# The first batch's chunk pairs interleaved in one pipeline, with idle products at the start and casts spread over engines

## The chip, the cores and the metric

The kernel runs on one core of one Trainium2 chip. The metric is device time in microseconds (us) of one execution; the figure given is the median of several runs. The core's engines work side by side, each through its own instructions in order: PE (TensorE, matrix products; PEld are its weight loads), DVE (VectorE), ACT (ScalarE), POOL (GpSimd) and SP, which here issues nearly all transfers (DMA).

## The reference

Four batches, 8 heads, 768 time steps, heads of 64. The first half is a retention layer (a linear attention with decay), the second a mixer with phases:

```python
gamma = 1.0 - 2.0 ** (-5.0 - np.arange(H))
for t in range(S):
    state = gamma * state + einsum('bhd,bhe->bhde', k[:, :, t], v[:, :, t])
    y[:, :, t] = scale * einsum('bhd,bhde->bhe', q[:, :, t], state)
x = y.transpose(0, 2, 1, 3).reshape(B, S, H * D)          # 4 x 768 x 512
theta = x @ w_theta
zr, zi = x * cos(theta), x * sin(theta)
u = x + einsum('ts,bsd->btd', w_tok_r, zr) + einsum('ts,bsd->btd', w_tok_i, zi)
out = u + maximum(u @ w_ch, 0)
```

## The kernel before

Time is cut into chunks of 128 steps: 6 a batch, 24 in all. Within a chunk the retention is a masked product; across chunks it is a running state. Chunk n's work has these stages, named as in the code:

- `prep`: k is cast to bf16, q and v are scaled by the decay (tiles kqb, vb), on POOL.
- `T`: PE transposes k and q (kq_ps), DVE copies them to kqT.
- `A`: PE forms the scores at_ps, DVE multiplies them with the mask into at. There is one at_ps buffer, so the next A waits for this mask.
- `Y`: PE multiplies at with v into yT_ps, and adds the product of the state (stbd) with q; the state's own product goes to st_ps, which ACT copies to stbd. ACT copies yT_ps to xT.
- `X`: PE transposes xT back (x_ps; DVE copies it to x_sb) and forms theta (th_ps); ACT takes cosine and sine (cs).
- `Z`: DVE forms z = x * (cos, sin).

When z of all six chunks of a batch is there, `moe_M` forms u for each of six output tiles (y_ps), `moe_U` transposes u, and `moe_O` multiplies with w_ch and stores. `w_cast` (POOL) casts a strip of both token weights to bf16 (wrow, three buffers), `w_tok` transposes it on PE (w_ps) and DVE and ACT copy it to wtr and wti.

The first batch is handled in three pairs of chunks: `load_pair` fetches 256 steps at once, two neighbouring steps to a row, and `pair_prep`, `pair_T`, `pair_A` and `pair_Y` take the place of the stages above; `two` counts the even and odd steps of a pair, `a` its two chunks. In `pair_Y` the two chunks' state products and readings are done one after the other. The other batches run one chunk to a slot, in the loop over `s_` at the end, with parts of `moe_M`, `moe_U` and `moe_O` between.

The order of the work on each engine is the order in which the code is written, since no scheduler moves anything (`manual_schedule`). Loads are queued in the order of one string, `loads("p0 th p1 w0 p2 w1 w2 c6 ...")` (p a pair, c a chunk, w a strip of the token weights, th and ch the two other weights); a load whose buffer is still in use holds up all behind it. PSUM has eight banks: two for at_ps, two with the tag "tr" (all transposes), two "acc" (yT_ps, th_ps, o_ps), one "y" (y_ps), one "st" (the state).

Of the kernel before, what the change touches and what calls it, by code (L numbers as in the profile page):

```python
# [14 lines left out]
FT = mybir.dt.float32  # L15
BF = mybir.dt.bfloat16
AF = mybir.ActivationFunctionType
# [4 lines left out]
def _bcast_last(ap: bass.AP, n: int) -> bass.AP:  # L22
    return bass.AP(tensor=ap.tensor, offset=ap.offset, ap=list(ap.ap) + [[0, n]])
# [9 lines left out]
def kernel(  # L33
# [17 lines left out]
    nc = tc.nc  # L51
    B, H, S, D = q.shape
    dm = H * D
    P = 128
    HP = P // 2
    nT = S // P
# [36 lines left out]
    wdma = {}  # L93
# [26 lines left out]
    loads("p0 th p1 w0 p2 w1 w2 c6 w3 c7 ch c8 w4 c9 c10 w5 c11 c12")  # L120


    posn = const.tile([P, nT], FT)
    nc.gpsimd.iota(posn, pattern=[[P, nT]], base=1, channel_multiplier=1,
                   allow_small_or_imprecise_dtypes=True)
# [22 lines left out]
    nc.scalar.activation(vscp, argp, AF.Exp, bias=zerob, scale=-1.0)  # L148
    qscp = const.tile([P, nT, H], FT)
    nc.scalar.activation(qscp, argp, AF.Exp, bias=lscale, scale=1.0)  # L150
    ident = const.tile([P, P], BF)
    make_identity(nc, ident)
    mask = const.tile([P, P], BF)
# [58 lines left out]
    def pair_prep(g, name):  # L212
        t = work.tile([P, 2, dm], BF, name="kqb", bufs=5)
        src = raw[g, name].rearrange("p h (two d) -> p two h d", two=2)
        dst = t.rearrange("p two (h d) -> p two h d", h=H)
        if name == "k":
            nc.gpsimd.tensor_copy(dst, src)
        else:
            for two in range(2):
                sc = (qscp if name == "q" else vscp)[:, 2 * g + two]  # L220
                nc.gpsimd.tensor_mul(dst[:, two], src[:, two], _bcast_last(sc, D))
        st[g, name] = t

    def pair_T(g, name):
        ps = psum.tile([P, NP, 2, P], BF, name="kq_ps", tag="tr", bufs=2)
        for two in range(2):
            for j in range(NP):
                nc.tensor.transpose(ps[:, j, two, :],
                                    st[g, name][:, two, j * P:(j + 1) * P], ident)
        t = work.tile([P, NP, 2, P], BF, name="kqT", bufs=4)  # L230
        nc.vector.tensor_copy(t, ps)
        st[g, name + "T"] = t
# [16 lines left out]
                             _bcast_mid(maskp[:, two].rearrange("p w i -> p (w i)"), H))  # L249
        st[g, two] = at  # L250

    def pair_Y(g):
        yT = [psum.tile([P, NP, P], FT, name="yT_ps", tag="acc", bufs=2)
              for _ in range(2)]
        for two in range(2):
            at, vp = st[g, two], st[g, "v"]
            for j in range(NP):
                for a in range(2):
                    half = slice(a * HP, (a + 1) * HP)
                    for par in range(2):  # L260
                        h = 2 * j + par
                        nc.tensor.matmul(yT[a][par * D:(par + 1) * D, j, :],
                                         vp[half, two, h * D:(h + 1) * D],
                                         at[half, par, j, :],
                                         start=(two == 0 and j == 0),
                                         stop=(g == 0 and a == 0 and two == 1
                                               and j == NP - 1),
                                         skip_group_check=True)
        for a in range(2):
            c = 2 * g + a  # L270
            half = slice(a * HP, (a + 1) * HP)
            if c > 0:
                for j in range(NP):
                    nc.tensor.matmul(yT[a][:, j, :], stbd[c % 2][:, j, :],
                                     st[g, "qT"][:, j, :, half], start=False,
                                     stop=(j == NP - 1), skip_group_check=True)
            if c < nT - 1:
                if c == 0:
                    st_ps[0] = psum.tile([P, NP, P], FT, name="st_ps", tag="st", bufs=1)
                for two in range(2):  # L280
                    for j in range(NP):
                        nc.tensor.matmul(st_ps[0][:, j, :],  # L282
                                         st[g, "k"][half, two, j * P:(j + 1) * P],
                                         st[g, "v"][half, two, j * P:(j + 1) * P],
                                         start=(c == 0 and two == 0 and j == 0),
                                         stop=(c == nT - 2 and two == 1 and j == NP - 1),
                                         skip_group_check=True)
                state_out(0, c)
            if c == 0:
                x_tiles(0)  # L290
            xT = work.tile([P, NP, P], BF, name="xT", bufs=3)
            nc.scalar.copy(xT.rearrange("e j (i w) -> e j w i", w=2),
                           yT[a].rearrange("e j (w i) -> e j w i", w=2))
            st[c] = dict(xT=xT)

    def state_out(b, c):
        for par in range(2):
            sl = slice(par * D, (par + 1) * D)
            nc.scalar.copy(stbd[(c + 1) % 2][sl, :, sl], st_ps[b][sl, :, sl])  # L299

    def x_tiles(b):
        xs[b] = big.tile([P, nT, dm], BF, name="x_sb")
        zs[b] = big.tile([P, nT, 2, dm], BF, name="z")
# [81 lines left out]
    def att_Z(n):  # L385
        b, c = divmod(n, nT)
        nc.vector.tensor_mul(zs[b][:, c], st[n]["cs"], _bcast_mid(xs[b][:, c, :], 2))  # L387
# [57 lines left out]
    def w_cast(t0):  # L445
        for r in range(2):
            row = work.tile([P, S], BF, name="wrow", bufs=3)
            nc.gpsimd.tensor_copy(row, wdma[r, t0])  # L448
            wrow[r, t0] = row

    def w_tok(t0):
        for r in range(2):
            w_ps = psum.tile([P, nT, P], BF, name="w_ps", tag="tr", bufs=2)
            for s0 in range(nT):
                nc.tensor.transpose(w_ps[:, s0, :],
                                    wrow[r, t0][:, s0 * P:(s0 + 1) * P], ident)
            dst = wT[r][:, :, t0 * P:(t0 + 1) * P]
            if r:
                nc.scalar.copy(dst, w_ps)
            else:  # L460
                nc.vector.tensor_copy(dst, w_ps)
# [47 lines left out]
                out=out[b, t0 * P:(t0 + 1) * P, e * hw:(e + 1) * hw], in_=ot)  # L509


    def pair_in(g):
        pair_prep(g, "k")
        pair_T(g, "k")
        pair_prep(g, "q")
        if g > 0:
            att_Z(2 * g - 1)
        pair_T(g, "q")
        pair_prep(g, "v")
        pair_A(g, 0)  # L520
        pair_A(g, 1)
        pair_Y(g)

    pair_in(0)
    nc.vector.tensor_copy(wth, wdma["th"])
    att_X(0)
    att_X(1)
    att_Z(0)
    pair_in(1)
    w_cast(0)  # L530
    att_X(2)
    w_tok(0)
    att_X(3)
    moe_M(0, 0, 2)
    att_Z(2)
    pair_in(2)
    moe_M(0, 2, 4)
    w_cast(1)
    att_X(4)
    w_tok(1)  # L540
    att_X(5)
    w_cast(2)
    att_prep(nT)
    moe_M(1, 0, 4)
    att_Z(4)
    moe_M(0, nT - 2, nT - 1)
    moe_M(1, nT - 2, nT - 1)
# [25 lines left out]
    for s_ in range(last_slot):  # L573
        n = n_of.get(s_)
        if n is not None and n + 5 < NCH and n >= nT + 2:
            load_chunk(n + 5)
        if U_at.get(s_, 0) >= M_DMA:
            moe_U_dma(U_at[s_])
        if n is not None and nT < n < N_DMA:
            att_T(n)  # L580
        if s_ - 3 in n_of:
            att_Z(n_of[s_ - 3])
        hs = halves.get(s_, [])
        if hs:
            moe_M(*hs[0])
        if s_ == 0:
            w_cast(3)
        if s_ in (2, 4):
            w_cast(3 + s_ // 2)
        if s_ + 1 in n_of and n_of[s_ + 1] < N_DMA:  # L590
            att_prep(n_of[s_ + 1])
        if s_ + 2 in n_of and n_of[s_ + 2] >= N_DMA:
            att_prep(n_of[s_ + 2])
            att_T_dma(n_of[s_ + 2])
        if U_at.get(s_, M_DMA) < M_DMA:
            moe_U(U_at[s_])
        if U_at.get(s_ - 1, 0) >= M_DMA:
            moe_O(U_at[s_ - 1])
        if s_ - 1 in n_of:
            att_Yinter(n_of[s_ - 1])  # L600
        if n is not None:
            att_A(n)
        if s_ - 1 in n_of:
            att_Y(n_of[s_ - 1])
            if n_of[s_ - 1] >= N_DMA:
                att_X_dma(n_of[s_ - 1])
        if s_ == 2:
            wch_cast(0, nD)
        if len(hs) > 1:
            moe_M(*hs[1])  # L610
        if s_ in O_at:
            moe_O(O_at[s_])
        if 1 < U_at.get(s_, M_DMA) < M_DMA:
            moe_O(U_at[s_])
        if s_ in (1, 3, 5):
            w_tok(3 + s_ // 2)
        if s_ - 2 in n_of:
            att_X(n_of[s_ - 2])
    moe_last(last_m)
# [28 lines left out]
```

## Time and profile before

| | us |
|---|---|
| median of 3 runs | 200.23 (200.01 to 200.25) |
| the profiled execution's own time | 199.73 |
| its span, first to last instruction | 197.9 |
| PE busy | 166.2 (84%) |
| DVE busy | 105.5 (53%) |
| ACT busy | 76.2 (39%) |
| POOL busy | 77.0 (39%) |

The span is what the profile shows instruction by instruction; the execution's own time is 1.83 us longer. Busy shares are means over the whole span. The page also cuts the span into 40 slices of 4.95 us and gives for each the busy share of every engine and the clock that PE was granted, in tenths of full speed.

### The profile page before, as it was taken

Reading aid. Unit: us, or ns where it says so; the run is one execution under the profiler, and the core shown is the slowest. Engines: PE = TensorE matmul, PEld = TensorE weight load, DVE = VectorE, ACT = ScalarE, POOL = GpSimd, SP = SyncE. Lnnn points to the kernel's source line nnn. Section 1 sums busy time; section 2 is a strip of 40 time slices with the busy share of each in tenths; the row PEclk is TensorE's granted clock in tenths of the full one; section 3 lists DMA queues with packets and bytes.
Section 4 is the critical chain, followed back from the end, with each engine's and each line's share of the span. In section 5 each row is a group of like instructions: output and inputs, shape, how many; then the busy total and the mean of one; then the engine's idle time right before and its main releaser. Section 6 shows DMA issues by size and latency. Waiting matters only on the chain.

```text
span 197.9 us, 3797 instructions
## 1 busy us (share of the span) xinstructions
PE 166.2 (84%) x1508; PEld 96.4 (49%) x1508; DVE 105.5 (53%) x147; ACT 76.2 (39%) x142; POOL 77.0 (39%) x107
## 2 busy tenths in 40 slices
PE   0448628945998997997999999999999999999990
PEld 0335416534554564654565566555555444444460
DVE  1162570462136747776787668666565554543451
ACT  4005703621531577536464464425643353200010
POOL 6849680300189882999255526525000000000000
PEclk9999985596799999999999999999999999999997
DMA  5999995199589999999496886994457445233343
GB/s 152 325 308 336 319 308 140 16 255 283 139 192 226 286 190 227 251 255 229 96 227 129 176 197 151 191 209 106 113 134 74 106 106 108 81 119 107 96 133 108
DMA packets 85906, 35.64 MB, mean 180 GB/s; under 512 B 70912, under 2 KB 80384, under 8 KB 85888
## 3 DMA queue, kind: packets, MB, share of 16 engines
q1 hardware_dynamic: 85744, 35.27, 76.5%
q8 instruction: 12, 0.20, 0.4%
q10 hardware_dynamic: 144, 0.13, 0.2%
q14 instruction: 6, 0.05, 0.1%
HBM read 25.69 MB, written 6.29 MB: 162 GB/s over the span
## 4 chain that ended last, share of the span: by engine, by line
PE 73%; DVE 11%; ACT 6%; DMA 3%; issue 2%; POOL 1%; DVEq 0%; SPq 0%; ACTq 0%; POOLq 0%
PE y_ps L405 29%; PE o_ps L433 10%; PE th_ps L376 10%; DVE at L247 4%; DMA pair<-in_q_dram 3%; PE yT_ps L340 3%; PE at_ps L311 3%; PE x_ps L373 2%; PE st_ps L282 2%; DVE z L387 2%; PE kq_ps L198 2%; PE st_ps L348 2%; DVE at L315 2%; ACT stbd L299 2%; PE at_ps L243 2%
## 5 line engine op out<-in xcount | busy, mean ns | idle before, releaser
L405 PE MATMUL y_ps<-z,wtr 128*128 128x512 bf16 x138 | 52.8, 383 | 1.0 <-DVE z L387 0.6
L405 PE MATMUL y_ps<-z,wti 128*128 128x512 bf16 x138 | 52.8, 383 | 0.0
L381 ACT ACTIVATE cs<-th_ps,halfpi 128x512 bf16<-128x512 f32 x24 | 16.5, 687 | 36.0 <-PE th_ps L376 36.0
L387 DVE TENSOR_TENSOR z<-cs,x_sb 128x1024 bf16<-128x1024 bf16 x24 | 19.7, 822 | 16.1 <-ACT cs L382 16.1
L376 PE MATMUL th_ps<-wth,xT 128*128 128x512 bf16 x96 | 27.3, 411 | 0.0
L299 ACT CAST stbd<-st_ps 64x256 bf16<-64x256 f32 x40 | 14.6, 366 | 30.3 <-PE st_ps L282 29.9
L315 DVE TENSOR_TENSOR at<-at_ps,mask 128x1024 bf16<-128x1024 f32 x18 | 21.9, 1219 | 5.7 <-PE at_ps L311 5.6
L433 PE MATMUL o_ps<-wch,uT 128*128 128x512 bf16 x92 | 23.4, 379 | 0.3 <-ACT cs L382 0.3
L410 DVE TENSOR_TENSOR u<-y_ps,x_sb 128x512 bf16<-128x512 f32 x23 | 15.8, 690 | 12.1 <-PE y_ps L405 12.0
L189 POOL TENSOR_TENSOR vb<-vf,vsc 128x512 bf16<-128x512 f32 x18 | 19.2, 1065 | 6.1 <-PE yT_ps L340 5.0
L436 DVE SCALAR_TENSOR_TENSOR ot<-o_ps,u 128x512 f32<-128x512 f32 x23 | 15.8, 690 | 9.8 <-PE o_ps L433 9.7
L405 PEld LDWEIGHTS <-wti 128*128 128x128 bf16 x138 | 13.6, 98 | 15.2 <-issue 2.4
L448 POOL CAST wrow<-wtok 128x768 bf16<-128x768 f32 x12 | 9.8, 823 | 28.7 <-issue 27.2
L405 PEld LDWEIGHTS <-wtr 128*128 128x128 bf16 x138 | 13.6, 98 | 13.6 <-issue 0.3
L187 POOL TENSOR_TENSOR kqb<-qf,qsc 128x512 bf16<-128x512 f32 x18 | 19.6, 1092 | 0.0
L186 POOL CAST kqb<-kf 128x512 bf16<-128x512 f32 x18 | 11.4, 634 | 19.0 <-issue 14.1
L379 DVE COPY x_sb<-x_ps 128x512 bf16<-128x512 bf16 x19 | 7.9, 418 | 18.0 <-PE x_ps L373 18.0
L382 ACT ACTIVATE cs<-th_ps,zerob 128x512 bf16<-128x512 f32 x24 | 16.3, 680 | 0.0
L356 ACT CAST xT<-yT_ps 128x512 bf16<-128x512 f32 x18 | 10.6, 586 | 11.9 <-PE yT_ps L340 11.7
L201 DVE COPY kqT<-kq_ps 128x1024 bf16<-128x1024 bf16 x13 | 9.0, 691 | 9.3 <-PE kq_ps L198 9.3
L433 PEld LDWEIGHTS <-uT 128*128 128x128 bf16 x92 | 8.8, 98 | 10.3 <-issue 0.6
L376 PEld LDWEIGHTS <-xT 128*128 128x128 bf16 x96 | 9.5, 107 | 8.0 <-issue 2.1
(73 smaller groups left out, 196.0 us busy)
## 6 DMA issues: line engine op xcount, KB each, us to landing
out_dram<-ot SPq DMA_DIRECT2D x23, 256.0 KB, 2.2
kf<-in_k_dram SPq DMA_DIRECT2D x18, 256.0 KB, 4.6
qf<-in_q_dram SPq DMA_DIRECT2D x18, 256.0 KB, 5.1
vf<-in_v_dram SPq DMA_DIRECT2D x18, 256.0 KB, 4.9
wtok<-in_moe_w_tok_r_dram SPq DMA_DIRECT2D x6, 384.0 KB, 5.4
wtok<-in_moe_w_tok_i_dram SPq DMA_DIRECT2D x6, 384.0 KB, 5.2
pair<-in_k_dram SPq DMA_DIRECT2D x3, 512.0 KB, 8.2
pair<-in_q_dram SPq DMA_DIRECT2D x3, 512.0 KB, 9.1
```

Of the source, the lines that this page charges most:

```text
L187: nc.gpsimd.tensor_mul(qb.rearrange(r3, h=H), raw[n, "qf"], _bcast_last(qsc[:, c], D))
L189: nc.gpsimd.tensor_mul(vb.rearrange(r3, h=H), raw[n, "vf"], _bcast_last(vsc[:, c], D))
L299: nc.scalar.copy(stbd[(c + 1) % 2][sl, :, sl], st_ps[b][sl, :, sl])
L315: nc.vector.tensor_mul(at.rearrange("p a j t -> p (a j) t"), at_ps.rearrange("p a j t -> p (a j) t"), _bcast_mid(mask, H))
L376: nc.tensor.matmul(th_ps, s["xT"][:, j, :], wth[:, j, :], start=(j == 0), stop=(j == NP - 1))
L381: nc.scalar.activation(cs[:, 0, :], th_ps, AF.Sin, bias=halfpi, scale=1.0)
L382: nc.scalar.activation(cs[:, 1, :], th_ps, AF.Sin, bias=zerob, scale=1.0)
L387: nc.vector.tensor_mul(zs[b][:, c], st[n]["cs"], _bcast_mid(xs[b][:, c, :], 2))
L405: nc.tensor.matmul(y_ps, wT[r][:, s0, t0 * P:(t0 + 1) * P], zs[b][:, s0, r, :], start=(s0 == 0 and r == 0), stop=(s0 == nT - 1 and r == 1))
L410: nc.vector.tensor_add(u, y_ps, xs[b][:, t0, :])
L433: nc.tensor.matmul(o_ps, mo[m]["uT"][:, j, :], wch[:, j, :], start=(j == 0), stop=(j == nD - 1))
L436: nc.vector.scalar_tensor_tensor(ot, o_ps, 0.0, mo[m]["u"], ALU.max, ALU.add)
```

## The change

1. Fourteen products of a zero tile (`warm`, 128x512) are put at PE's start; their result is not used. DVE clears the tile with its first instruction.
2. A single sine on one column (`sin0`) is put behind the exponentials, so that ACT loads its sine table there.
3. k of a pair is cast on ACT instead of POOL; q's first half is scaled on DVE, its second still on POOL; w_theta is cast on POOL instead of DVE.
4. `pair_Y` is split: `pair_Y(g, two)` has the products with v of one half, `pair_I` the state's reading, `pair_S` the state's product, `pair_out` the copy to xT. They are written in another order, S and Y of a pair between its two masks, and `att_X`, `att_Z` and `moe_M` of earlier chunks stand between the stages of the next pair.
5. In the slots `w_tok` stands ahead of `att_Yinter`, `att_A` and `att_Y` instead of behind them, and `moe_U` behind `att_Yinter`.

```diff
-    pair_in(0)
-    nc.vector.tensor_copy(wth, wdma["th"])
+    warm_ps = psum.tile([P, dm], FT, name="y_ps", tag="y", bufs=1)
+    for _ in range(14):
+        nc.tensor.matmul(warm_ps, warm[:, 0:P], warm, start=True, stop=True)
+    pair_k(0)
+    pair_q(0)
+    pair_prep(0, "v")
+    pair_A(0, 0)
+    nc.gpsimd.tensor_copy(wth, wdma["th"])
+    pair_A(0, 1)
+    pair_S(0, 0)
+    pair_Y(0, 0)
+    pair_S(0, 1)
+    pair_I(0, 1)
+    pair_Y(0, 1)
+    pair_out(0, 0)
+    pair_out(0, 1)
+    pair_k(1)
     att_X(0)
+    pair_q(1)
     att_X(1)
     att_Z(0)
-    pair_in(1)
+    pair_prep(1, "v")
+    pair_A(1, 0)
+    att_Z(1)
     w_cast(0)
+    pair_A(1, 1)
+    pair_S(1, 0)
+    pair_Y(1, 0)
+    pair_I(1, 0)
+    pair_I(1, 1)
+    pair_S(1, 1)
+    pair_Y(1, 1)
+    pair_out(1, 0)
+    pair_out(1, 1)
+    pair_prep(2, "k")
     att_X(2)
+    att_X(3)
     w_tok(0)
-    att_X(3)
+    pair_T(2, "k")
     moe_M(0, 0, 2)
+    pair_q(2)
     att_Z(2)
-    pair_in(2)
-    moe_M(0, 2, 4)
+    pair_prep(2, "v")
+    pair_A(2, 0)
+    moe_M(0, 2, 3)
+    att_Z(3)
     w_cast(1)
+    pair_A(2, 1)
+    pair_S(2, 0)
+    pair_Y(2, 0)
+    pair_I(2, 0)
+    pair_I(2, 1)
+    moe_M(0, 3, 4)
+    pair_Y(2, 1)
+    pair_out(2, 0)
+    pair_out(2, 1)
+    w_tok(1)
     att_X(4)
-    w_tok(1)
-    att_X(5)
     w_cast(2)
     att_prep(nT)
     moe_M(1, 0, 4)
+    att_X(5)
     att_Z(4)
...
+        if s_ in (1, 3, 5):
+            w_tok(3 + s_ // 2)
...
         if s_ - 1 in n_of:
             att_Yinter(n_of[s_ - 1])
+        if U_at.get(s_, M_DMA) < M_DMA:
+            moe_U(U_at[s_])
```

`pair_k(g)` is `pair_prep(g, "k")` and `pair_T(g, "k")`, and `pair_q(g)` the same for q. The new casts:

```diff
         if name == "k":
-            nc.gpsimd.tensor_copy(dst, src)
...
+            nc.scalar.copy(dst, src)
+        for two in range(2):
+            if name == "q":
+                eng = (nc.vector, nc.gpsimd)[two]
...
```

ACT from its last exponential to the sines of the first two chunks, before. The buffer's number stands behind each name; xT_328 and xT_344 are chunks 0 and 1.

```order
L150 ACTIVATE qscp_189<-argp_185,lscale_171 128x48
L299 CAST stbd1_207<-st_ps_315 64x4x64 x2
L292 CAST xT_328<-yT_ps_281 128x4x2x64
L299 CAST stbd0_205<-st_ps_315 64x4x64 x2
L292 CAST xT_344<-yT_ps_282 128x4x2x64
L381 ACT_TABLE_LOAD
L381 ACTIVATE cs_358<-th_ps_352,halfpi_173 128x512
```

The same place after the change; kqb_232 and kqb_366 are k of the first and the second pair.

```order
L152 ACTIVATE qscp_191<-argp_187,lscale_173 128x48
L154 ACT_TABLE_LOAD
L154 ACTIVATE sin0_193<-zerob_177 128x1
L221 CAST kqb_232<-pair_72 128x1024
L318 CAST stbd1_211<-st_ps_301 64x4x64 x2
L318 CAST stbd0_209<-st_ps_301 64x4x64 x2
L295 CAST xT_362<-yT_ps_312 128x4x2x64
L295 CAST xT_364<-yT_ps_313 128x4x2x64
L221 CAST kqb_366<-pair_80 128x1024
L400 ACTIVATE cs_390<-th_ps_384,halfpi_175 128x512
```

The table load has moved ahead of the first k cast, and the second pair's k cast stands behind both xT of the first.

DVE in the second pair, before: z_327 are the first two chunks' z, at_424 and at_443 the two masks.

```order
L387 TENSOR_TENSOR z_327<-cs_358,x_sb_326 128x1024
L231 COPY kqT_387<-kq_ps_378 128x1024
L387 TENSOR_TENSOR z_327<-cs_372,x_sb_326 128x1024
L231 COPY kqT_402<-kq_ps_393 128x1024
L247 TENSOR_TENSOR at_424<-at_ps_407,maskp_199 128x1024
L247 TENSOR_TENSOR at_443<-at_ps_426,maskp_199 128x1024
```

And after:

```order
L239 COPY kqT_377<-kq_ps_368 128x1024
L398 COPY x_sb_360<-x_ps_379 128x512
L225 TENSOR_TENSOR kqb_393<-pair_82,qscp_191 128x512
L239 COPY kqT_405<-kq_ps_396 128x1024
L398 COPY x_sb_360<-x_ps_407 128x512
L406 TENSOR_TENSOR z_361<-cs_390,x_sb_360 128x1024
L255 TENSOR_TENSOR at_442<-at_ps_425,maskp_203 128x1024
L406 TENSOR_TENSOR z_361<-cs_418,x_sb_360 128x1024
L255 TENSOR_TENSOR at_466<-at_ps_449,maskp_203 128x1024
```

The copies of k and q no longer stand behind a z, but each mask does, and q's half is new between them.

DVE in slot 5, before: wtr_211 is the last copy of token weights.

```order
L410 TENSOR_TENSOR u_1239<-y_ps_1130,x_sb_326 128x512
L315 TENSOR_TENSOR at_1260<-at_ps_1251,mask_196 128x1024
L461 COPY wtr_211<-w_ps_1278 128x6x128
L379 COPY x_sb_884<-x_ps_1294 128x512
L201 COPY kqT_1323<-kq_ps_1314 128x1024
```

And after:

```order
L429 TENSOR_TENSOR u_1258<-y_ps_1149,x_sb_360 128x512
L480 COPY wtr_215<-w_ps_1265 128x6x128
L334 TENSOR_TENSOR at_1295<-at_ps_1286,mask_200 128x1024
L398 COPY x_sb_919<-x_ps_1313 128x512
L205 COPY kqT_1342<-kq_ps_1333 128x1024
```

The copy of the weights has changed places with the mask.

## What is predicted

> **What bounds the kernel now.** I read the slices first, then a table by stage.
>
> ```profile
> PE   0448628945998997997999999999999999999990
> PEclk9999985596799999999999999999999999999997
> ...
> 0.00:20.00 20.00, 8.65 (x107) 6.03 (x108) 6.34 (x10) 5.19 (x11) 14.20 (x37) 1.00 1.01 281
> 20.00:40.00 20.00, 13.71 (x146) 8.99 (x145) 8.36 (x11) 9.20 (x16) 8.86 (x10) 0.74 0.73 194
> 40.00:60.00 20.00, 14.06 (x162) 8.96 (x161) 7.90 (x11) 6.48 (x12) 5.77 (x7) 0.83 0.92 219
> 60.00:100.00 40.00, 36.43 (x387) 22.23 (x387) 28.08 (x40) 20.82 (x40) 29.84 (x34) 1.00 1.02 219
> 100.00:150.00 50.00, 50.00 (x450) 28.47 (x449) 33.66 (x46) 24.70 (x49) 18.35 (x21) 1.00 0.80 160
> ```
>
> In the slices each digit is a fortieth of the span, 4.95 us; 9 means nine tenths or more. In the table the window is followed by its length, the busy time of PE, weight loads, DVE, ACT and POOL, the granted clock, DMA's share and GB/s. From 100 us on PE is never idle; from 60 to 100 it lacks 3.57 us of 40; before 60 it is idle for 23.6 us (60 less 8.65, 13.71 and 14.06), and part of the rest runs at half clock. So the front is paced by waits, the rest by PE, and a product that starts earlier at the seam moves the end by as much. The waits of PE say what paces the front:
>
> ```profile
> PE at_ps L243 <- DVE kqT L231: 5.3, 3, 3.0
> PE at_ps L243 <- DVE at L247: 4.1, 3, 1.4
> PE yT_ps L262 <- DVE at L247: 3.2, 3, 1.1
> PE x_ps L373 <- DVE wtr L461: 1.6, 2, 1.3
> PE x_ps L373 <- ACT wti L459: 0.9, 1, 0.9
> ```
>
> The first three are the pairs' ping-pong: copy, product, mask, product, with PE idle meanwhile. The last two belong to the token weights. The columns are the total, how often, and the longest. The chain that ended last gives the milestones and PE's prices; its two th_ps rows, four equal products each, give half and full clock (427 and 215 ns each).
>
> ```profile
> 10.38 0.67 PE at_ps L243 x16
> ...
> 20.05 1.28 ACT L381
> 21.34 0.69 ACT cs L381
> 22.03 0.59 ACT cs L382
> ...
> 26.17 0.44 PE at_ps L243 x16
> ...
> 34.82 1.71 PE th_ps L376 x4
> ...
> 39.49 0.86 PE y_ps L405 x4
> 40.35 0.46 PE kq_ps L228 x8
> ...
> 42.78 0.44 PE at_ps L243 x16
> ...
> 47.44 0.98 PE st_ps L282 x8
> ...
> 49.31 0.61 PE yT_ps L274 x4
> ...
> 54.50 0.86 PE th_ps L376 x4
> ...
> 60.28 0.61 PE y_ps L405 x2
> ```
>
> The seam is 60.28, the first product with the sixth chunk's z. What follows is the same work in both kernels, but for w_tok's place.
>
> **The change, part by part.** Prices of the other engines (count, busy us, mean ns), and four places in time:
>
> ```profile
> L387 DVE TENSOR_TENSOR z<-cs,x_sb 128x1024 bf16<-128x1024 bf16 x24 | 19.7, 822 | 16.1 <-ACT cs L382 16.1
> L247 DVE TENSOR_TENSOR at<-at_ps,maskp 128x1024 bf16<-128x1024 f32 x6 | 7.3, 1224 | 3.7 <-PE at_ps L243 3.7
> L231 DVE COPY kqT<-kq_ps 128x1024 bf16<-128x1024 bf16 x6 | 4.1, 686 | 8.0 <-PE kq_ps L228 8.0
> ...
> L299 ACT CAST stbd<-st_ps 64x256 bf16<-64x256 f32 x40 | 14.6, 366 | 30.3 <-PE st_ps L282 29.9
> L292 ACT CAST xT<-yT_ps 128x512 bf16<-128x512 f32 x6 | 4.4, 731 | 0.1
> L459 ACT COPY wti<-w_ps 128x768 bf16<-128x768 bf16 x6 | 4.8, 798 | 4.3 <-PE w_ps L455 4.2
> L441 ACT CAST wch<-w 128x512 bf16<-128x512 f32 x4 | 2.2, 615 | 0.0
> ```
> ```profile
> 3.63 0.32 ACT L150 ACTIVATE qscp<-argp,lscale 128x48 f32<-128x48 f32 x1
> 5.07 1.04 POOL L217 CAST kqb<-pair 128x1024 bf16<-128x1024 f32 x1 [1.08 <-DMA pair<-in_k_dram]
> 6.89 2.04 POOL L221 TENSOR_TENSOR kqb<-pair,qscp 128x512 bf16<-128x512 f32 x2 [0.78 <-DMA pair<-in_q_dram]
> 13.13 1.04 POOL L217 CAST kqb<-pair 128x1024 bf16<-128x1024 f32 x1 [2.20 <-DMA pair<-in_k_dram]
> 18.82 1.91 PE L376 MATMUL th_ps<-wth,xT 128*128 128x512 bf16 x4
> 24.21 1.31 DVE L387 TENSOR_TENSOR z<-cs,x_sb 128x1024 bf16<-128x1024 bf16 x1
> ```
>
> k cast on ACT is not shown: between 0.80 (wti, fewer columns) and 1.23 (two wch); I take 1.0. q half on DVE: 0.5 (half a kqT copy, rounded up) to 1.31 (z beside POOL); I take 0.9, 0.7 where POOL rests. At each change of engine I add an estimated 0.05. State products at full clock are half of 0.98; a y product block (Y) costs what at_ps does.
>
> Idle products: at 18.82 the th_ps row lasts 1.91, which is the half-clock figure, though PEclk reads 9 there; so the array is cold until about 21. Fourteen products take 3.0 (all at 215 ns) to 6.0 us (all at 427) from about 1.3, when DVE has cleared their operand. They end at 4.3 to 7.3, while k is ready at 6.6: between 0 and 0.7 us of delay, I take 0. No row shows whether products of zeros wake the clock. If they don't, pair 0 runs at half clock as before: two transposes (0.54 each) and an at_ps (0.23) dearer ahead of the first mask, 1.3 us; if they do, nothing; I take nothing, since the clock row answers to busy PE everywhere else.
>
> *Pair 0.* ACT ends its scales at 3.95; the sine table, now loaded here instead of at 20.05 (1.28), and its one trial sine (0.32, as the scale) add 1.6; the k cast runs 5.6 to 6.6, half a microsecond later than POOL's. Transposes 0.46 and kqT 0.69 bring 7.9; DVE's q half 0.9, transposes 0.46, kqT 0.69: first at_ps at 10.1 against 10.38. The mask runs twice, to 13.6; beneath it lie the state products S, the first half's Y and again S, which waits for stbd (two by 366); Y of the second half ends at 15.3. Before, nothing of this lay beneath the masks but the first Y.
>
> *Pair 1.* Two xT (1.46) stand ahead of the k cast on ACT: it ends at 17.8, though k landed by 13.13. That is what is late next. I let the clock fall here, since from 13.2 to 17.8 PE works about a quarter of the time. Cold transposes 1.0, cold x and th 2.2, which bring 21.1 (DVE makes q's half beneath them), then warm again q's transposes 0.46 and x and th 1.1: at_ps at 22.6, not 26.17. Each mask now waits behind a z on DVE (0.9): the masks end at 24.8 and 26.9; S, Y, the two state readings I (0.23 each warm) and S fill PE meanwhile, and the last Y ends at 27.8.
>
> *Seam to pair 2.* stbd, two xT: 29.65. x and th of two chunks, w_tok: PE done at 31.9. ACT has the k cast (30.65), four sines (2.56; 33.2) and wti (0.8): first y_ps product at 34.1, not 39.49.
>
> *Pair 2.* y_ps 0.86, q transposes 0.46, kqT 0.69: at_ps at 36.2, not 42.78. z 0.7 and mask 1.22, then the second at_ps at 38.1; S, Y, I, I, y_ps and Y end at 41.0; before, this pair's last product ends at 49.9.
>
> *To the seam.* w_tok 0.7; two xT and wti on ACT to 43.3; the second row's products 1.72, x and th 1.1, ending at 46.2; sines 1.28; kqT stands ahead of z on DVE; z ends 49.3. Seam at 49.34: 10.9 earlier. The same addition over the rows of before gives 61.4 for its 60.28, so it is good to about 1 us. Without the cold stretch it is 48.3; with a second one, through w_tok and the sines at 29 to 36, 51.6.
>
> *w_tok earlier in slots 1, 3, 5.* The copies no longer stand right ahead of x_ps, which waited for them 0.9 and 1.3 us (longest of each kind). Gain 0 to 2.2; I take 1.5, since the mask of that slot now stands 0.5 behind wtr.
>
> *Costed at nothing.* The theta cast on POOL, twice 1.04: theta is queued ahead of the k that lands by 13.13, the cast ends by 15.3, th needs it at 19.4; without that cover the excess counts once. SP: the third v load reuses k's buffer and now waits for ACT's cast, 17.8 instead of 14.2; all loads behind it wait too, but q of pair 2 only starts to be used at 33. DMA's 0.73 from 20 to 40 leaves room for that.
>
> Sum: span 197.9 − 10.9 − 1.5 = 185.5; the profiled run adds 1.83 outside its span (199.73), the median of the runs stands 0.5 above it: 187.8.
>
> [...] The clock at 23.2 to 28.5 and 40.9 to 45.5:
>
> ```profile
> 23.20:28.50 5.30, 1.02 (x49) 0.87 (x49) 4.26 (x6) 0.56 (x1) 4.57 (x5) 1.00 1.08 354
> 40.90:45.50 4.60, 1.40 (x55) 1.04 (x52) 3.56 (x5) 0.00 (x0) 0.00 (x0) 1.00 1.21 266
> ```
>
> Right behind each stretch the slices show half clock, though PE had worked 19% and 30%. Hence my cold stretch after pair 0. [...]
>
> DVE's z took 1.31 us beside POOL, against 0.82 on average; so I priced z and q's half at 0.9. [...]
>
> **The rivals.**
> - *Cold throughout.* The front's products are short with gaps, and the trace throttles at 30% work. Every step above at half clock (0.66 for at_ps, 1.71 for th) puts the seam at 63.3: 60.28 plus 3.0, less 1.5, so 201.7, slower. It decides once nearly nine tenths of the front is cold (15 us lie between 48.3 and 63.3, and 13.5 of them use up the gain). Against it: in the slices the clock comes up twice before 60 although PE waits more there than in my walk.
> - *Half the gain lost.* A second cold stretch (51.6), no gain from w_tok, DVE held by POOL on each q and z (0.5 each, four on the path): 197.9 − 8.7 + 2 + 2.3 = 193.5.
> - *Loads pace what follows, so that interleaving moves waits only.* From 60 to 100 DMA's share is 1.02: nothing to spare. What can be drawn forward is what DMA left idle, 0.27 of 20 us and 0.08 of 20: 7.0 us. The other 5.4 of the 12.4 would come back as waits for loads: 193.2. Against it: among PE's waits none is for a load, so loads land ahead of use, and that lead is used up first.
> - *All warm*, w_tok's whole 2.2: 197.9 − 12.0 − 2.2 + 2.3 = 186.0.
>
> **Numbers.** Forecast 187.8 (186.5 to 190): 0.62. All warm, 185 to 186.5: 0.12, with a little of it below. Half the gain lost, 190 to 194: 0.12. Loads: 0.08. Cold throughout, or losses that I don't name: 0.06. Only the last ends on the other side. The range 185 to 192 leaves out 0.2: the last, most of the loads, the upper half of the third, and a little below. A change of 0.2% is about what these runs can tell: faster 0.93, same 0.02, slower 0.05.
>
> **What would show it.** The first y_ps product with the sixth z near 49; at_ps of the pairs at 10, 22.6 and 36; the clock row at 5 for one or two slices, not five; the k cast near 1.0 on ACT behind two xT; x_ps no longer waiting for wtr. I am wrong if the clock row stays at 5 into slice 8, if ACT's casts take twice 1.0, or if PE is idle after the seam for loads that before came in time.

## The result

The changed kernel takes 191.68 us (median of 4 runs, 190.94 to 192.86) against 200.16: a ratio of 0.958 (95% interval 0.952 to 0.964). The forecast was 187.8 in a range of 185 to 192. Ratios leave out runs more than 1.5% above a kernel's fastest. The profiled run took 191.03, its span is 189.3.

The changed kernel's slices and stages, in the columns of before:

```profile
PE   7645966869878969999999999999999999999991
PEclk9985596978999999999999999999999999999999
...
0.00:20.00 20.00, 12.41 (x127) 7.33 (x128) 6.42 (x11) 8.49 (x15) 11.86 (x34) 0.83 1.00 280
20.00:40.00 20.00, 14.38 (x171) 8.73 (x173) 11.91 (x17) 9.43 (x16) 7.14 (x7) 0.83 0.88 231
40.00:60.00 20.00, 16.88 (x179) 10.39 (x181) 10.63 (x16) 6.97 (x12) 12.38 (x15) 0.91 1.06 243
60.00:100.00 40.00, 38.07 (x409) 24.02 (x411) 28.89 (x41) 24.23 (x47) 28.60 (x32) 1.00 1.05 223
```

PE is still idle for 16.3 us of the first 60 (23.6 before), though 5.6 us of its work there are idle products; and the clock row dips three times. Milestones on PE, and what ended the wait ahead of each:

```profile
10.29 0.42 PE L251 MATMUL at_ps<-kqT 64*64 64x128 bf16 x16 [0.78 <-DVE kqT L239]
...
18.35 1.03 PE L236 MATMUL kq_ps<-ident,kqb 128*128 128x128 bf16 x8 [2.31 <-ACT kqb L221]
...
24.10 0.42 PE L251 MATMUL at_ps<-kqT 64*64 64x128 bf16 x16
...
30.32 0.61 PE L392 MATMUL x_ps<-ident,xT 128*128 128x128 bf16 x4 [1.31 <-ACT xT L295]
...
38.58 0.42 PE L251 MATMUL at_ps<-kqT 64*64 64x128 bf16 x16 [0.78 <-DVE kqT L239]
...
53.20 0.38 PE L424 MATMUL y_ps<-z,wtr 128*128 128x512 bf16 x1 [0.60 <-DVE z L406]
```

The three pairs' at_ps start at 10.3, 24.1 and 38.6 (predicted 10.1, 22.6, 36.2; before 10.4, 26.2, 42.8). The seam is at 53.20, not 49.34: 7.1 us earlier than before instead of 10.9. From the seam to the span's end it is 136.1 us, before 137.6: those 1.5 us are the size predicted (w_tok's place alone, below, gives 0.9). So the loss against the forecast lies ahead of the seam. PE's waits (total, times, longest):

```profile
PE at_ps L251 <- DVE at L255: 3.5, 3, 1.4
PE kq_ps L236 <- ACT kqb L221: 2.3, 1, 2.3
PE kq_ps L236 <- DVE kqb L225: 1.8, 2, 1.6
PE at_ps L251 <- DVE kqT L239: 1.6, 2, 0.8
PE u_ps L435 <- ACT wti L478: 1.5, 1, 1.5
PE x_ps L392 <- ACT xT L295: 1.3, 1, 1.3
```

The wait for kqT has fallen from 5.3 to 1.6, that of Y for the masks is gone; new are the waits for k's cast on ACT (2.3) and q's half on DVE (1.8, where q on POOL cost 1.2). In steps of 3.41 us, the clock (third figure from the end) looks like this:

```profile
9.57:12.98 3.41, 1.29 (x40) 0.97 (x39) 2.23 (x3) 0.00 (x0) 2.72 (x3) 1.00 1.15 326
12.98:16.40 3.42, 2.79 (x46) 1.98 (x44) 0.89 (x1) 1.79 (x5) 1.61 (x2) 0.51 1.21 301
16.40:19.81 3.41, 1.46 (x13) 1.41 (x14) 0.39 (x1) 1.89 (x3) 2.67 (x3) 0.50 1.09 344
19.81:23.22 3.41, 2.95 (x16) 1.71 (x16) 2.28 (x4) 1.26 (x2) 0.97 (x2) 0.50 1.23 292
...
26.64:30.05 3.41, 2.14 (x52) 1.41 (x48) 1.66 (x2) 1.98 (x5) 2.19 (x2) 1.00 1.12 270
30.05:33.46 3.41, 2.92 (x13) 1.72 (x15) 0.79 (x2) 2.50 (x5) 0.00 (x0) 0.51 0.81 192
...
36.88:40.29 3.41, 1.60 (x26) 1.10 (x27) 2.69 (x5) 0.00 (x0) 0.00 (x0) 1.00 1.05 261
40.29:43.70 3.41, 3.37 (x49) 2.49 (x49) 1.80 (x2) 0.73 (x2) 0.00 (x0) 0.51 1.10 285
```

Each change falls on a border of this grid: down at 13.0, 30.05 and 40.3, up at 23.2, 33.5 and 43.7, 17 us at half clock in all. I had allowed for one stretch, over by 21.1.

### The profile page after: what moved, and what is told of

Read it like the earlier page. It is cut to its first block, busy times and chain, and to the rows that moved or that the text cites. A ratio compares the mean times of both kernels' runs of the same rounds, so it can differ in the third digit from the quotient of the medians.

```text
span 189.3 us, 3807 instructions
## 1 busy us (share of the span) xinstructions
PE 166.2 (88%) x1496; PEld 95.6 (51%) x1522; DVE 106.5 (56%) x150; ACT 78.9 (42%) x146; POOL 73.1 (39%) x102
## 4 chain that ended last, share of the span: by engine, by line
PE 79%; DVE 8%; ACT 5%; issue 4%; DMA 2%; DVEq 0%; ACTq 0%
PE y_ps L424 29%; PE o_ps L452 10%; PE th_ps L395 10%; PE yT_ps L359 3%; PE at_ps L330 3%; PE y_ps L542 3%; PE kq_ps L202 3%; PE x_ps L392 3%; PE st_ps L367 2%; PE kq_ps L236 2%; PE st_ps L307 2%; DVE at L255 2%; PE yT_ps L348 2%; PE u_ps L435 2%; DMA uT<-u 2%
## 5 line engine op out<-in xcount | busy, mean ns | idle before, releaser
L424 PE MATMUL y_ps<-z,wti 128*128 128x512 bf16 x135 | 51.2, 379 | 1.0 <-ACT wti L478 0.2
L424 PE MATMUL y_ps<-z,wtr 128*128 128x512 bf16 x126 | 48.0, 381 | 1.4 <-DVE z L406 1.0
L406 DVE TENSOR_TENSOR z<-cs,x_sb 128x1024 bf16<-128x1024 bf16 x24 | 19.0, 793 | 15.1 <-ACT cs L401 15.1
L395 PE MATMUL th_ps<-wth,xT 128*128 128x512 bf16 x89 | 26.0, 402 | 0.7 <-issue 0.4
L455 DVE SCALAR_TENSOR_TENSOR ot<-o_ps,u 128x512 f32<-128x512 f32 x23 | 15.9, 692 | 10.5 <-PE o_ps L452 10.4
L190 POOL CAST kqb<-kf 128x512 bf16<-128x512 f32 x18 | 11.4, 635 | 19.6 <-issue 10.4
L401 ACT ACTIVATE cs<-th_ps,zerob 128x512 bf16<-128x512 f32 x24 | 16.3, 679 | 0.0
L452 PEld LDWEIGHTS <-uT 128*128 128x128 bf16 x92 | 8.8, 98 | 10.2 <-DMA uT<-u 0.4
```

The lines of the kernel that those rows point to most:

```text
L395: nc.tensor.matmul(th_ps, s["xT"][:, j, :], wth[:, j, :], start=(j == 0), stop=(j == NP - 1))
L401: nc.scalar.activation(cs[:, 1, :], th_ps, AF.Sin, bias=zerob, scale=1.0)
L424: nc.tensor.matmul(y_ps, wT[r][:, s0, t0 * P:(t0 + 1) * P], zs[b][:, s0, r, :], start=(s0 == 0 and r == 0), stop=(s0 == nT - 1 and r == 1))
L452: nc.tensor.matmul(o_ps, mo[m]["uT"][:, j, :], wch[:, j, :], start=(j == 0), stop=(j == nD - 1))
L455: nc.vector.scalar_tensor_tensor(ot, o_ps, 0.0, mo[m]["u"], ALU.max, ALU.add)
```

## The experiments

Two theories stood against each other: that half clock cost the missing 3.9 us, or that new waits on ACT and DVE did, with the clock of no account. All compared kernels were timed in batches, each beside the kernel before, whose median was 199.5 to 200.3 from batch to batch; between batches the ratios are compared.

**Zero products in the gaps (clock up, waits as they are).**

```diff
+    idle(2)
     pair_A(0, 0)
+    idle(4)
...
+    idle(8)
     pair_k(1)
...
     pair_A(1, 0)
+    idle(4)
...
+    idle(5)
     pair_prep(2, "k")
...
+    idle(3, mo[0]["y"])
     pair_A(2, 0)
     moe_M(0, 2, 3)
+    idle(3, mo[0]["y"])
```

> The changed kernel with 29 more products of the zero tile, put where PE waited in its front: 2 and 4 around the first pair's first at_ps, 8 ahead of the second pair's k, 4 behind its first at_ps, 5 ahead of the third pair, 3 and 3 around the third pair's first at_ps (these add zeros to y_ps). Clock theory (most of the 3.9 us by which the seam came later than predicted is work at half clock, in three stretches of 3 to 10 us): the clock row stays at 9 through the front, the seam comes at 50 to 51 instead of 53.2, time about 188.5. Hand-off theory (waits on ACT's casts and DVE's half of q set the front, PE's speed lies beneath them): clock up, but the seam moves by less than 0.8, time 190.3 to 191.5.

Measured: 185.37 us, ratio 0.928 (0.925 to 0.930). Its clock row, and the seam on PE's timeline:

```profile
PEclk9999999999999999999999999999999999999998
```
```profile
47.95 0.38 PE L424 MATMUL y_ps<-z,wtr 128*128 128x512 bf16 x1 [0.60 <-DVE z L406]
```

No slice ahead of the last (8 tenths) shows a fall of the clock, and the seam comes 5.3 us earlier, more than the clock theory had asked for. All that was added is work without use. The prediction's walk gave 48.3 for a front without a cold stretch; the chip gives 47.95, and at_ps of the three pairs starts at 10.05, 21.35 and 34.38, where the walk less its cold 1.0 us has 10.1, 21.6 and 35.2. The four runs lie within 0.65 us of each other, the changed kernel's within 1.9.

**k and q of the later pairs on POOL (waits away, no products added).**

```diff
-            nc.scalar.copy(dst, src)
+            (nc.scalar.copy if g == 0 else nc.gpsimd.tensor_copy)(dst, src)
...
-                eng = (nc.vector, nc.gpsimd)[two]
+                eng = (nc.vector, nc.gpsimd)[two] if g == 0 else nc.gpsimd
```

> The changed kernel with k of the second and third pair cast on POOL, and both halves of their q scaled on POOL; the first pair as changed. Hand-off theory: the second pair's k no longer waits behind two xT on ACT (2.3 us of PE's wait there), the third pair's q no longer behind DVE's kqT (0.7): seam near 50.2, time about 188.5. Clock theory: the gap closes, but what was at half clock stays so, since the clock had fallen at 13 us, before that gap; gain 1 us or less, time 190 to 191.

Measured: 186.06, ratio 0.934 (0.930 to 0.938), again more than either theory's figure. The second pair's k on POOL's timeline, its transposes and the seam on PE's, and two stretches of the grid:

```profile
13.25 1.04 POOL L224 CAST kqb<-pair 128x1024 bf16<-128x1024 f32 x1
```
```profile
16.16 1.04 PE L239 MATMUL kq_ps<-ident,kqb 128*128 128x128 bf16 x8
...
48.14 0.38 PE L427 MATMUL y_ps<-z,wtr 128*128 128x512 bf16 x1 [0.60 <-DVE z L409]
```
```profile
13.00:16.40 3.40, 3.13 (x50) 2.23 (x48) 0.64 (x1) 1.60 (x5) 2.64 (x4) 0.50 1.20 303
16.40:19.80 3.40, 3.18 (x28) 2.23 (x27) 1.06 (x3) 1.68 (x3) 3.40 (x4) 0.61 1.10 343
```

k is cast when it lands instead of 4 us later, and PE has no wait ahead of it. From 16.4 to 19.8 PE is busy for 3.18 us, not 1.46, and the clock is back at 19, not at 23.2. This fits one chain of the two theories: the wait on ACT opens a gap, the clock, which fell before it, stays down in the gap, and slow products stretch what follows. The chain is not shown by this trace alone, since its grid lies elsewhere (the clock falls at 12.2, not 13.0); the next run bears on it.

**Only k to POOL, q split as changed.**

> The changed kernel with only k of the second and third pair on POOL; q's halves stay split between DVE and POOL. If k behind two xT on ACT was the loss: within 0.7 of the run with both on POOL, 186 to 187. If DVE's half of q was: 189.5 or more.

Measured: 186.61, ratio 0.932 (0.928 to 0.936). It was k: two casts of 1.05 us, moved from ACT to POOL, take off 5 us. For q's halves no difference is shown (medians 0.5 apart, intervals that overlap). The profiled run is one of this kernel's two longest (188.34); its clock row, and the seam from its chain:

```profile
PEclk9965796969999999999999999999999999999998
```
```profile
50.45 0.61 PE y_ps L427 x2
```

Here the clock stood at half for 17 us in three stretches, as long as in the changed kernel, the first of them 10.2 us though PE had no wait for k. And yet the seam is 2.7 us earlier than 53.20. So the wait for k costs some 2.7 us with the clock just as low, and a gap is not all that keeps the clock down. The rest of the 5 us goes with a clock that was low for less time: the four shorter runs have means of 0.961 to 0.981, the changed kernel's 0.938 to 0.955.

**Both edits together (e1 and e2).**

> Both edits of the first two experiments together: zero products in PE's gaps, and the second and third pair's k and q on POOL. If the two losses are separate (each took 5 us off): seam near 45 and 181 to 182.5. If they are largely one loss (the wait for k on ACT made the gap in which the clock stayed low): seam at 46.5 to 47.5 and 183.5 to 185.

Measured: 184.05, ratio 0.923 (0.920 to 0.926), seam at 46.28. Each edit alone took off 5.6 to 6.3, both 7.6: largely one loss, as the second expectation has it.

**The interleaved order alone.** Casts as before (k and q on POOL, theta on DVE behind the first pair's second at_ps), no idle products, no early sine, w_tok and moe_U in their old places.

```diff
-    for _ in range(14):
-        nc.tensor.matmul(warm_ps, warm[:, 0:P], warm, start=True, stop=True)
...
-    nc.gpsimd.tensor_copy(wth, wdma["th"])
     pair_A(0, 1)
+    nc.vector.tensor_copy(wth, wdma["th"])
```

> The interleaved order alone: casts on POOL and theta on DVE as before, no idle products, no early sine, w_tok in its old place. If the order is what pays and the casts' spread costs: seam at 50 to 52 and 188.5 to 191, no slower than the whole change (191.7). If the parts that are left out carry a good part: 193 or more.

Measured: 188.00, ratio 0.944 (0.940 to 0.948), better than the whole change and than either expectation. Its profiled run, the fastest (186.52), has products at full speed from 19.4 us on (eight transposes in 0.61 us, not 1.03) and the seam at 47.4 (from its page and its chain):

```profile
PEclk9999999999999999999999999999999999999997
```
```profile
47.40 0.61 PE y_ps L423 x2
```

As in the kernel before, the 9s at the row's start stand over cold products (its at_ps takes 0.66 us at 10.41).

**The changed kernel with all k and q on POOL.**

> The changed kernel with all of k and q on POOL, the first pair's too (theta's cast stays on POOL). The order alone took 188.0, w_tok's place took 0.9 by itself, and the pairs after the first gave 5.6 us: 186.5 to 187.5 if those add and the first pair's spread is worth little; if the first pair's spread pays (its q ready 1 us earlier), 187.5 to 188.5 and slower than the run with only the later pairs on POOL (186.1).

Measured: 186.35, ratio 0.934 (0.930 to 0.937), the same as with only the later pairs there. Spreading k and q costs 5 us in this order, and no gain in the first pair is shown either.

**Idle products alone, on the kernel before.**

> The kernel before, with only the fourteen idle products at the start. If they pay by themselves: the first pair's products and the first two th_ps at full clock, at least 1.5 us, time below 198.9. If the clock falls back before the first pair is through, as in the changed kernel at 13 us: within 0.5 us of before, first at_ps 0.5 earlier at most.

Measured: 200.41 against 200.27, ratio 1.001 (0.998 to 1.003). Nothing: the first pair's at_ps runs at full speed (0.42 us, before 0.64), but the clock falls back in the third slice, and the second pair's at_ps starts at 26.03 (before 26.17), since its wait for kqT has grown from 3.0 to 3.9.

```profile
PEclk9985965795599999999999999999999999999998
```

**The changed kernel with one idle product instead of fourteen.**

> The changed kernel with one idle product instead of fourteen. By the run with idle products alone they are worth nothing: 191 to 192.5. If they matter in the interleaved order, because pair 0 then starts at full clock: 193 to 194.

Measured: 192.81, between the two expectations, but with a spread of 5.3 us: from 188.85 to 194.16, the same instructions. The ratio, 0.949 (0.944 to 0.955), rests on two of the six runs; by the median of all six it would be 0.967. Whether the fourteen pay in the new order is not shown.

**Six more zero products, around the first pair's first at_ps only.**

> The changed kernel with only 6 more zero products, 2 and 4 around the first pair's first at_ps, ahead of the first fall of the clock at 13 us. If one fall leads to the next (cold products stretch the front and open the later gaps): clock at 9 past 16 us, two falls instead of three, 188 to 190. If each fall is set by its own gap: the clock falls at 16.4 instead of 13, in the 2.3 us wait for k, and the time stays within 1 us of 191.7.

Measured: 189.0, ratio 0.944 (0.940 to 0.948): 2.7 us for 6 products. The seam of the profiled run is at 51.4. Its clock row:

```profile
PEclk9997596999999999999999999999999999999999
```

The time and the two falls instead of three (at 16.0 and 29.65) are the first expectation's; that the clock falls at 16.0 all the same, in the wait for k, is near the second's. It stood at half for 10.2 us, not 17. How much of this is owed to where the grid lay in this run is not shown.

**w_tok's new place alone, on the kernel before (moe_U moves with it).**

```diff
+        if s_ in (1, 3, 5):
+            w_tok(3 + s_ // 2)
         if U_at.get(s_ - 1, 0) >= M_DMA:
```

> The kernel before, with only the new places of w_tok and moe_U in the slots. The prediction's term: 1.5 us (0 to 2.2) from x_ps' waits for wtr and wti, time 198.7. Rival: the waits move on to u_ps, which takes the same two banks next (2.1 us of u_ps waits in the changed kernel's trace): nothing gained, 200.0 to 200.4.

Measured: 199.35, ratio 0.996 (0.994 to 0.998): 0.9 us. PE's waits there:

```profile
PE u_ps L416 <- ACT wti L459: 1.5, 1, 1.5
...
PE u_ps L416 <- DVE wtr L461: 0.6, 1, 0.6
PE x_ps L373 <- DVE wtr L461: 0.5, 2, 0.3
```

x_ps' 1.6 and 0.9 have become 0.5, and u_ps, which takes the same banks next, has 2.1 of its own.

**No early sine (on the kernel with both edits).**

> The kernel with zero products in the gaps and later k and q on POOL (184.05), without the early sine. The sine table's 1.28 us then stand ahead of the first sines, near 18 to 20 us, where x and th of the first chunks are through. If that is on the path: 185.0 to 185.5. If PE has other work there: k's cast 0.5 us earlier instead, 183.6 to 184.3.

Measured: 184.08 against 184.05. The early table load is worth nothing there.

**w_ch's casts ahead of the slots (on the same kernel).**

```diff
     moe_M(1, nT - 1, nT)
+    wch_cast(0, nD)
...
-        if s_ == 2:
-            wch_cast(0, nD)
```

> The kernel with zero products in the gaps and later k and q on POOL (184.05), with the four casts of w_ch on ACT moved from slot 2 to ahead of the slots. Their 2.18 us stand there ahead of two sines and wti, on which u_ps waits 1.5 us, in every kernel with the new place of w_tok. If that wait is what they cost: u_ps waits no more and 182.5 to 183.0. If the wait moves on (to the next tr bank, or to loads): above 183.5.

Measured: 183.74, ratio 0.918 (0.916 to 0.921), the fastest of all, though no more than 0.3 below its parent, with intervals that overlap. The wait for wti is gone and one for wtr has grown in its place:

```profile
PE u_ps L438 <- DVE wtr L483: 1.6, 2, 1.0
```

## Why the prediction was right, and where it was off

- *What bounds the kernel.* Right: from the seam on PE sets the pace, and a seam 5.3 us earlier (zero products) gave 5.7 us at the end of the profiled span (183.6 against 189.3).
- *The term that was mis-sized is the clock.* "I let the clock fall here" gave pair 1 one cold stretch, over by 21.1 (1.0 us on the path). The trace has 17 us in three: at_ps of pair 1 is 1.5 us late, of pair 2 2.4, and the seam 3.9, one step more for each stretch. The all-warm walk itself was good to 0.4 us at the seam. I weighed PE's share of work in stretches of my own choosing; in the trace the changes stand on a grid of 3.41 us, and the clock fell behind a stretch 63% busy (26.64 to 30.05), where I had no fall.
- *k on ACT.* Priced right (1.03 to 1.05, I took 1.0) and named as late next, with a clock that falls there but is up again at 21.1. In the kernel it cost 5 us: some 2.7 with the clock as low as in the changed kernel, the rest with the time at half clock.
- *q's half on DVE.* 0.87, 1.34 and 0.68 where I took 0.9, 0.9 and 0.7; 1.34, beside a POOL cast (20.33 to 21.16), is just above my upper end of 1.31. In pair 0 the two halves overlap: POOL's ran from 7.24 to 8.28 and DVE's from 7.97 to 8.84, and at_ps is 0.2 late. In sum no loss is shown.
- *Idle products.* The fourteen ended at 6.87, within the range of 4.3 to 7.3, and do wake the clock though they multiply zeros, as I had taken it (at_ps at 10.29 in 0.42 us, before 0.64); on the kernel before they gain nothing at the end.
- *w_tok.* 1.5 in the profiled pair of spans, 0.9 by itself (I gave 0 to 2.2). The waits moved to u_ps, which I had not named.
- *Costed at nothing.* Theta's cast on POOL took 1.89 from 11.66, hidden. SP's third v load waited to 18.32 (15.41 before); the loads kept ahead, and with zero products the gain reached the end in full, so loads did not pace what follows.
- *The rivals.* The second cold stretch was there, and a third. 191.68 lies outside the forecast's own band (186.5 to 190) and in the one of "Half the gain lost" (190 to 194), to which I gave 0.12. That rival's seam of 51.6 was not late enough either; but w_tok did gain, and no loss by DVE is shown. Cold throughout did not happen. The range held by 0.3 us, and two of the four runs lie above it: that is luck.
- *The waits ahead of the falls.* In the 3.41 us ahead of each of the three falls PE's longest wait was 1.4 us (10.71 to 12.11), and the clock fell.

What stays open: what the falls and rises at the grid's borders go with. In the changed kernel the clock stayed up after a stretch with 2.09 us of work (23.22 to 26.64) and fell after one with 2.14. The rises don't go with PE's busy time alone either: with only k on POOL the clock stayed down after a step with 3.38 us of mostly short products (14.20 to 17.61), while in the changed kernel it rose after one with 2.92 us, mostly of 512 columns (30.05 to 33.46).

## What to carry to other kernels

When short products with waits between them make up a stage, look at the granted clock in the steps in which the traces show it change (3.41 us here), not only at the waits: here a wait of 2.3 us on PE went with a loss of 5. Put a cast on the engine that is free when its data lands, not on the one with the fewest busy microseconds (the later pairs' k on POOL instead of ACT: 5 us less); where a gap can't be closed, products of zeros can keep the clock up: 29 of them, six added as zeros to a bank in use, gained 6 us at the end. Time the order of the work and its spread over engines apart: here the order alone gave 188.0, all of the change 191.7.

## What the runs showed of the hardware

The granted clock's changes stand whole steps of 3.41 us apart, within 0.1 (changed kernel: 13.0, 23.2, 30.05, 33.5, 40.3, 43.7; before: 28.5, 38.7, 45.5, 52.4; later pairs' k and q on POOL: 12.2, 19.0, 36.1, 39.5), and where the grid lies differs from trace to trace. Runs of one and the same kernel spread by 2.6 and 2.7 us with their mean clock (all k and q on POOL: 184.83 at 0.979, 187.47 at 0.960; only the later pairs' on POOL: 185.78 at 0.967, 188.44 at 0.950); that the place of the grid is the reason is a guess of mine, not shown. The four kernels whose mean clock was 0.987 or more in every run spread by 0.7 to 1.7 us. Products of zeros hold the clock too: with 29 of them no slice of the front shows a fall. In the trace of before the granted clock reads full speed from the start to its first fall at 28.5, while products near its start take half-clock times (at_ps in 0.64 us at 10.38, in 0.42 with the fourteen idle products ahead; four th_ps in 1.91 us at 18.82, in 1.03 at 54.34).
